# A projection matrix folded four row tiles at a time, output columns in two equal halves, and a new hand-written order of steps

## The chip, the cores and the metric

One Trainium2 chip, one core. The metric is the device time of one execution in microseconds (us). Kernels are compared by the median of several executions. The core's engines run side by side, each through a queue of its own in order: TensorE (PE in the rows; PEld is its weight load), VectorE (DVE), ScalarE (ACT), GpSimd (POOL), and SyncE (SP), whose queue issues the DMAs.

## The reference

Three stages follow one another; r, k, v, w are (4 batches, 8 heads, 768 steps, 48), w_in and w_out come in float64.

```
# 1 attention with a decaying state, per batch and head
y[t] = r[t] @ (state + (u*k[t]) v[t]^T);  state = w[t]*state + k[t] v[t]^T
x = y as (3072 tokens, 384)
# 2 a wide layer
h = x @ w_in          # 384 -> 2048
g = h * cos(h)
x2 = g @ w_out        # 2048 -> 384
# 3 soft mixture of 8 experts with 4 slots each
logits = x2 @ phi                          # 384 -> 32
d = softmax(logits, over tokens);  slot_in = d.T @ x2
slot_out[e] = relu(slot_in[e] @ w1[e]) @ w2[e]
out = softmax(logits, over slots) @ slot_out   # (3072, 384)
```

## The kernel before, in words

**Stages.** x2 itself is never formed. The kernel computes p = w_out @ phi once (2048 x 32, `p_sb`), so that logits are g @ p, and it gathers d.T @ g (`E`, 32 x 2048) and multiplies that by w_out at the end. Attention runs over 24 blocks of 128 tokens (`wT`, `wf`, `scan`, `kT`, `ks`, `rT`, `L`, `A`, `mask`, `U`, `z`, `st`, `y`; the number behind a step's name is the block). The wide layer runs over 12 groups of 256 tokens and 8 blocks of 256 hidden columns: `h.g.i.mm` is one 128-column half of block i in group g, of nine f32r matmuls (L451 to L453: high and low parts of x and w_in). `turns`, `rest`, `cos`, `mul` (ACT, DVE, ACT, DVE) make g, `gT` transposes it, `gc` copies it, `l` adds to the logits. A block of h waits for the `mul` of the block two before it, whose bank it takes.

**The fold and the decode.** The float64 weights are read as pairs of integers and turned into float32 by `abs`, `mx`, `d1`, `d2a`, `d2b` (one on ACT, four on DVE; `i` is w_in, `o` is w_out, each in 8 pieces). For w_out each of 16 row tiles m is then transposed (`oT.m`, L416, three 128x128 pieces), copied to SBUF (`oc.m`, L421, ACT) and multiplied by phi (`om.m`, L427): the transposed tile is the stationary operand, and phi's 32 columns move. All sixteen results lie in one PSUM bank `pp`, held from the first `om` to the last `ps` (L430, ACT), which copies four tiles of it to `p_sb`.

**The order.** A string `HEAD` of some 1980 steps gives the order in which the steps are issued, and with it each engine's queue. Nothing reorders it later. It starts with attention and decode and ends with the last `E`.

**The tail.** After `HEAD` come the slots, then for each expert `hidden` (w1) and `expert_out` (w2, L826, by four column groups of 32 slots), then `slots_out` (L833), `slots_round`, and `outputs` (L857 for 512 tokens in f32, L859 for the others in f32r), whose result is copied from PSUM to `ob` (L866 and L873) and sent (L867). This is done for two parts of the 384 columns: 256, then 128. Five of the w2 weights (`we`) are issued late, into buffers that the wide layer frees.

Of the kernel before, what the change touches and what calls it, by code (L numbers as in the profile page):

```python
# [902 lines left out]
A.0 z.0.1 mask.0 wn.0.0 raw.o.0 st.0.1 lk.2 kT.1 rz.0.1 rz.0.0 lv.1 mx.o.3 d1.o.3 ks.1 d2a.o.3 wn.0.1 wc.0.1 d2b.o.3 lw.2 y.0 lz.2
abs.o.0 lr.2 lw.3 z.1.0 lv.2 A.1 yb.0 mx.o.0 d1.o.0 abs.o.2 mx.o.2 wc.0.0 kN.1 ksn.1 d2a.o.0 d2b.o.0 oT.1 xh.0 xl.0 d1.o.2 raw.i.1
abs.o.1 mx.o.1 d1.o.1 oT.0 oc.0 oc.1 om.0 d2a.o.1 d2a.o.2 wT.2 wf.2 d2b.o.1 om.1 lz.1 raw.i.4 mask.1 d2b.o.2 oT.3 oT.2 oc.2 oc.3
U.1 ru.1 bo.1 oT.4 rz.1.0 abs.i.1 st.1.0 z.1.1 rz.1.1 st.1.1 bv.1 scan.2 kT.2 abs.i.4 om.2 ks.2 y.1 yb.1 om.3 mx.i.4 xh.1 xl.1
mx.i.1 d1.i.1 d2a.i.1 kN.2 d2b.i.1 h.0.2.0 h.0.2.1 ksn.2 oc.4 rT.2 sr.2 sp.2 L.2 raw.i.3 lr.3 lw.4 d1.i.4 z.2.0 d2a.i.4 d2b.i.4
whi.1 wn.1.0 h.0.0.0 wc.1.0 h.0.0.1 turns.0.0 rz.2.0 oT.5 wT.3 oc.5 rest.0.0 ru.2 bo.2 bv.2 U.2 wf.3 A.2 cos.0.0 wn.1.1 st.2.0
turns.0.2 wc.1.1 mul.0.0 gT.0.0 om.4 lk.3 kT.3 mask.2 z.2.1 st.2.1 scan.3 ks.3 rest.0.2 whi.4 abs.i.3 mx.i.3 d1.i.3 sr.3 d2a.i.3
d2b.i.3 sp.3 wn.4.0 kN.3 ksn.3 wn.4.1 h.0.1.0 h.0.1.1 wc.4.0 lw.5 raw.i.6 abs.i.6 lv.4 whi.3 gc.0.0 lk.4 mx.i.6 cos.0.2 wc.4.1  # L910
wn.3.0 oT.7 wc.3.0 rT.3 wn.3.1 raw.i.5 d1.i.6 rz.2.1 oc.7 y.2 wc.3.1 d2a.i.6 turns.0.1 abs.i.5 mul.0.2 L.3 A.3 wT.4 h.0.3.0
d2b.i.6 wf.4 mx.i.5 d1.i.5 z.3.0 whi.6 mask.3 wn.6.1 ps.0 wc.6.1 rest.0.1 scan.4 yb.2 om.5 cos.0.1 xh.2 kT.4 d2a.i.5 ru.3 lk.5
wn.6.0 mul.0.1 sr.4 lv.3 ks.4 l.0.1 xl.2 sp.4 d2b.i.5 U.3 st.3.0 raw.i.7 abs.i.7 z.3.1 mx.i.7 oT.6 wc.6.0 gT.0.2 gc.0.2 lr.5 bo.3
st.3.1 d1.i.7 oc.6 d2a.i.7 h.0.3.1 gT.0.1 wT.5 wf.5 kN.4 h.0.4.0 gc.0.1 d2b.i.7 lz.3 whi.7 wn.7.0 whi.5 h.0.4.1 wn.5.1 lr.4
raw.o.5 bv.3 turns.0.3 rest.0.3 rz.3.0 scan.5 ksn.4 wn.5.0 turns.0.4 rest.0.4 wc.7.0 raw.o.4 lz.4 abs.o.4 mx.o.4 wc.5.0 wc.5.1
rz.3.1 ru.5 bo.5 rT.4 L.4 cos.0.4 om.7 ru.4 wn.7.1 lr.6 om.6 cos.0.3 d1.o.4 d2a.o.4 mul.0.3 ps.1 wc.7.1 abs.o.5 U.4 z.4.0 rz.4.0
st.4.0 z.4.1 st.4.1 rz.4.1 d2b.o.4 y.3 mul.0.4 l.0.3 A.4 yb.3 xh.3 kT.5 ks.5 mask.4 h.0.5.0 xl.3 h.0.5.1 lw.6 lk.6 raw.o.6 rT.5
mx.o.5 lz.5 d1.o.5 turns.0.5 kN.5 ksn.5 sr.5 rest.0.5 oT.8 gT.0.3 oc.8 oT.9 sp.5 d2a.o.5 gc.0.3 bo.4 oc.9 d2b.o.5 cos.0.5 h.0.7.0
h.0.7.1 lv.5 bv.5 turns.0.7 wT.6 om.9 wf.6 mul.0.5 gT.0.5 rest.0.7 L.5 oT.11 raw.o.7 U.5 A.5 oc.11 om.11 z.5.0 scan.6 st.5.0
abs.o.6 mx.o.6 z.5.1 lw.7 abs.o.7 d1.o.6 d2a.o.6 st.5.1 rz.5.1 om.8 cos.0.7 z.6.0 d2b.o.6 mul.0.7 h.0.6.0 h.0.6.1 wT.7 oT.10  # L920
h.1.1.0 h.1.1.1 mask.5 tab turns.0.6 gc.0.5 rest.0.6 gT.0.4 kT.6 cos.0.6 oc.10 sr.6 sp.6 mul.0.6 ks.6 oT.13 oc.13 rz.5.0 om.10
gc.0.4 ps.2 wf.7 rT.6 mx.o.7 d1.o.7 h.1.0.0 oT.12 oc.12 d2a.o.7 d2b.o.7 close l.0.5 om.13 oT.14 oT.15 om.12 turns.1.1 bv.4 ru.6
# [136 lines left out]
```

## Time and profile before

| | before |
|---|---|
| median of 3 runs | 566.48 us (565.99 to 566.79) |
| profiled execution | 567.16 us |
| its span, first to last instruction | 565.4 us |
| mean granted TensorE clock | 0.975 |
| PE busy, share of the span | 516.0 us, 91% |
| DVE busy | 438.7 us, 78% |
| ACT busy | 313.3 us, 55% |
| POOL busy | 123.2 us, 22% |
| read from HBM, written | 61.75 MB, 4.72 MB |

The span leaves out 1.76 us of the execution's own time. Busy shares are means over the span; the start, the long middle and the tail have different limits, so that a change is weighed in its own stretch. A granted clock of 1.00 is 2.4 GHz, one of 0.50 is 1.2 GHz.

### The profile page before, as it was taken

The numbers are of one execution on the slowest core, as the hardware profiler recorded it, in microseconds if no ns is written. First come the engines' busy times: TensorE is split into PE (matmuls) and PEld (weight loads), VectorE is DVE, ScalarE is ACT, GpSimd is POOL, SyncE is SP. The second block draws the span as 40 slices with busy tenths as digits, with TensorE's granted clock in tenths as the row PEclk, the third lists the DMA queues.
The fourth block names the chain that finished last, engine by engine and source line by source line (L and its number), as shares of the span: only waits on it lengthen the run. The fifth ranks groups of instructions, "written<-read, shape, count | busy, mean of one in ns | idle before, by whom it ended". The sixth has DMA issues, their size and how long they took to land.

```text
span 565.4 us, 16220 instructions
## 1 busy us (share of the span) xinstructions
PE 516.0 (91%) x6846; PEld 447.6 (79%) x6846; DVE 438.7 (78%) x823; ACT 313.3 (55%) x657; POOL 123.2 (22%) x163
## 2 busy tenths in 40 slices
...
GB/s 206 297 167 88 144 179 126 128 71 16 112 55 75 68 33 58 44 72 43 45 86 39 61 16 90 41 106 51 59 59 12 6 225 378 180 237 225 405 202 275
DMA packets 146712, 67.52 MB, mean 119 GB/s; under 512 B 127568, under 2 KB 134736, under 8 KB 146640
## 3 DMA queue, kind: packets, MB, share of 16 engines
...
HBM read 61.75 MB, written 4.72 MB: 118 GB/s over the span
## 4 chain that ended last, share of the span: by engine, by line
PE 58%; DVE 27%; ACT 6%; DMA 4%; issue 3%; SPq 0%; DVEq 0%; ACTq 0%
PE h L451 9%; PE h L453 8%; PE h L452 8%; PE gT L483 5%; PE l L496 3%; PE y L288 3%; PE E L592 3%; DVE g L475 3%; DMA we<-in_moe_w_dram 3%; PE A L208 3%; DVE L L222 3%; DVE g L467 3%; DVE L L187 2%; PE U L259 2%; DVE qt L156 2%
## 5 line engine op out<-in xcount | busy, mean ns | idle before, releaser
L451 PE MATMUL h<-x,wu 128*128 128x256 f32 x573 | 168.8, 295 | 3.9 <-DVE g L475 3.6
L453 PE MATMUL h<-x,wu 128*128 128x256 f32 x573 | 162.3, 283 | 0.0
L452 PE MATMUL h<-x,wu 128*128 128x256 f32 x573 | 162.3, 283 | 0.0
L451 PEld LDWEIGHTS h<-x,wu 128*128 128x128 f32 x573 | 110.3, 193 | 6.1 <-DVE g L475 5.2
L452 PEld LDWEIGHTS h<-x,wu 128*128 128x128 f32 x573 | 110.4, 193 | 0.2
L453 PEld LDWEIGHTS h<-x,wu 128*128 128x128 f32 x573 | 110.0, 192 | 0.0
L471 ACT ACTIVATE g<-g,half_pi 128x512 f32<-128x512 f32 (+1 forms) x97 | 69.2, 718 | 44.0 <-DVE g L467 43.4
L463 ACT ACTIVATE g<-h 128x512 int32<-128x512 f32 x96 | 56.9, 595 | 59.1 <-PE h L453 39.1
L467 DVE SCALAR_TENSOR_TENSOR g<-g,h 128x512 f32<-128x512 int32 x96 | 64.9, 678 | 27.5 <-ACT g L463 26.8
L475 DVE TENSOR_TENSOR g<-g,h 128x512 f32<-128x512 f32 x96 | 64.7, 678 | 22.9 <-ACT g L471 22.2
L251 POOL TENSOR_TENSOR bv<-vz,bo 64x384 f32<-64x384 f32 x48 | 41.9, 873 | 151.8 <-DVE bo L243 56.6
L488 ACT COPY gt<-gT 128x512 f32<-128x512 f32 x92 | 53.4, 584 | 28.5 <-PE gT L483 22.5
L483 PE MATMUL gT<-cs,g 128*128 128x128 f32 x384 | 58.9, 278 | 2.4 <-DVE g L475 1.7
L169 POOL TENSOR_TENSOR ru<-rn,u_b 128x384 f32<-128x384 f32 x24 | 27.7, 1156 | 123.2 <-DVE bo L243 46.0
L483 PEld LDWEIGHTS gT<-cs,g 128*128 128x128 f32 x384 | 43.6, 142 | 12.3 <-issue 6.5
L274 ACT COPY rzs<-z 64x192 f32<-64x192 f32 x96 | 33.4, 348 | 9.5 <-DVE z L269 8.4
L156 DVE TENSOR_TENSOR_SCAN qt<-wf,one_b 128x520 f32<-128x520 f32 x24 | 31.9, 1329 | 6.5 <-ACT wf L151 6.4
L187 DVE TENSOR_TENSOR L<-rT,pt 64x512 f32<-64x512 f32 x48 | 32.9, 686 | 4.3 <-PE y L288 2.8
L222 DVE TENSOR_TENSOR L<-A,cs 64x512 f32<-64x512 f32 x48 | 33.1, 689 | 1.2
L193 POOL MEMSET L<- 64x512 f32 x32 | 16.6, 520 | 69.3 <-PE y L288 68.3
L496 PE MATMUL l<-g,p_sb 128*32 128x256 f32 x384 | 29.8, 385 | 1.5 <-DVE g L475 1.5
L164 DVE TENSOR_TENSOR_SCAN pt<-wf,ini_f 128x520 f32<-128x520 f32 x24 | 30.2, 1258 | 0.2
...
## 6 DMA issues: line engine op xcount, KB each, us to landing
...
```

The lines of the kernel that those rows point to most:

```text
L187: nc.vector.tensor_tensor(out=L[h, a], in0=ps[h], in1=segs(pt, 0, C)[h], op=ALU.mult)
L222: nc.vector.tensor_tensor(out=L[h, a], in0=ps[h], in1=mask[h].unsqueeze(1).to_broadcast([64, NS, C]), op=ALU.mult)
L451: nc.tensor.matmul(hp, lhsT=wh, rhs=xh[:, c, :], start=(c == 0), stop=False)
L452: nc.tensor.matmul(hp, lhsT=wh, rhs=xl[:, c, :], start=False, stop=False)
L453: nc.tensor.matmul(hp, lhsT=wl, rhs=xh[:, c, :], start=False, stop=(c == KD - 1))
L463: nc.scalar.activation(gt.bitcast(I32), hp, AF.Copy, bias=0.25, scale=1.0 / TWO_PI)
L467: nc.vector.scalar_tensor_tensor(out=gt, in0=gt.bitcast(I32), scalar=-TWO_PI, in1=hp, op0=ALU.mult, op1=ALU.add)
L471: nc.scalar.activation(gt, gt, AF.Sin, bias=half_pi[:, 0:1])
L475: nc.vector.tensor_tensor(out=gt, in0=gt, in1=hp, op=ALU.mult)
L483: nc.tensor.transpose(ps[:, tt, mm, :], gt[:, mm, tt * 128:(tt + 1) * 128], ident)
L488: (nc.vector.tensor_copy if NBK * g + i >= ATT and i in (1, 2) else nc.scalar.copy)(t, pend.pop(("gT", g, i)))
L496: nc.tensor.matmul(lps_t[g][32 * mm:32 * mm + 32, 0:G], lhsT=p_sb[:, m, :], rhs=g_t[g, m // 2][:, m % 2, :], start=(m < 4), stop=(m >= MF ...
```

## The change

Three things, of which the first two can be seen in the code. **The fold**: `om.u` now takes four row tiles at once. phi is the stationary operand (32 columns), the transposed w_out tile moves with its 128 columns, and the four tiles go to four column groups of the array, which write four quarters of the partitions of a bank `pt` of their own. The result is p transposed, so that two steps follow: `pc` (copy to SBUF, ACT) and `pT` (one transpose); `ps` then copies as before. The transposed tiles lie in the pool of 12 buffers that also holds the copied `gT`. **The tail**: `halves` of 192 columns each take the place of the parts of 256 and 128, the second half's `expert_out` stands alternately with the first half's `outputs`, and the second half's output is stored for every pair of token tiles. **The order**: `HEAD` is another list, of 1977 steps.

```diff
     def e_oc(m):
-        wt_t[m] = aw.tile([128, KD, 128], F32, tag="wt", name=f"wt{m}")
+        wt_t[m] = gt_p.tile([128, KD, 128], F32, tag="gt", name=f"wt{m}")
         nc.scalar.copy(wt_t[m], pend.pop(("woT", m)))
-    def e_om(m):
-        if not pt_ps:
-            pt_ps[0] = ps_m.tile([128, MF, SL], F32, tag="m", name="pp")
+    def e_om(u_):
+        ps = ps_m.tile([128, 512], F32, tag="m", name=f"pt{u_}")
         for c in range(KD):
-            nc.tensor.matmul(pt_ps[0][:, m, :], lhsT=wt_t[m][:, c, :], rhs=phi_sb[:, c, :], start=(c == 0), stop=(c == KD - 1))
+            for q in range(4):
+                nc.tensor.matmul(ps[32 * q:32 * q + 32, 0:128], lhsT=phi_sb[:, c, :], rhs=wt_t[4 * u_ + q][:, c, :], start=(c == 0), stop=(c == KD - 1))
+        pt_ps[u_] = ps
+    def e_pc(u_):
+        wt_t["p", u_] = aw.tile([128, 128], F32, tag="pts", name=f"pts{u_}", bufs=1)
+        nc.scalar.copy(wt_t["p", u_], pt_ps[u_][:, 0:128])
+    def e_pT(u_):
+        pend["P", u_] = tps(f"P{u_}")[:, 0:128]
+        nc.tensor.transpose(pend["P", u_], wt_t["p", u_], ident)
     def e_pw(u_):
-        nc.scalar.copy(p_sb[:, 4 * u_:4 * u_ + 4, :], pt_ps[0][:, 4 * u_:4 * u_ + 4, :])
+        nc.scalar.copy(p_sb[:, 4 * u_:4 * u_ + 4, :], pend.pop(("P", u_)).rearrange("p (q s) -> p q s", q=4))
...
         parts = (slice(0, 256), slice(256, DM))
+        halves = (slice(0, DM // 2), slice(DM // 2, DM))
...
             def expert_out(i, e):
-                cols = parts[i]
+                cols = halves[i]
...
             def outputs(i, n0, tile_=None):
-                cols = parts[i]
+                cols = halves[i]
...
             outputs(0, 1, 0)
             outputs(0, 1, 1)
-            for n0 in range(2, 5):
-                outputs(0, n0)
-            for e in range(1, 4):
+            outputs(0, 2)
+            for e in range(1, NE):
+                outputs(0, e + 2)
                 expert_out(1, e)
-            for n0 in range(5, 9):
-                outputs(0, n0)
-            for e in range(4, NE):
-                expert_out(1, e)
-            nc.vector.tensor_copy(so[:, parts[1]], ops[1][:, 0:128])
-            for n0 in range(9, 12):
-                outputs(0, n0)
+            nc.vector.tensor_copy(so[:, halves[1]], ops[1][:, 0:DM // 2])
+            outputs(0, NE + 2)
             slots_out(1)
+            outputs(0, NE + 3)
             slots_round(1)
-            for n0 in range(6):
+            for n0 in range(12):
                 outputs(1, n0)
...
-z.0.0 lw.0 wT.0 wf.0 scan.0 raw.i.0.0 abs.i.0.0 mx.i.0.0 sr.0 d1.i.0.0 sp.0 raw.i.2 abs.i.2 mx.i.2 raw.i.0.1 abs.i.0.1 lw.1 wT.1
+lw.0 wT.0 wf.0 scan.0 sr.0 lk.0 sp.0 lr.0 kT.0 ks.0 rT.0 lw.1 wT.1 wf.1 raw.i.0.0 abs.i.0.0 raw.i.2 abs.i.2 z.0.0 L.0 A.0 scan.1
```

What the new list does to a queue is shown at three places. In these rows a name is followed by its tile's number. First DVE, where the start ends: the rows around `mul.0.7` (the product that writes `g0_7`, for which `h.1.1.0` waits). Before:

```order
L269 TENSOR_TENSOR z5_0_1335<-st_state_130,qt5_1034 128x192
L156 SCALAR_TENSOR_TENSOR qt6_1337<-wf_127,one_b_128 128x520
L277 TENSOR_TENSOR st_state_130<-U5_1304,z5_0_1335 128x192
L357 TENSOR_SCALAR ao6_1340<-ao6_1340 128x768
L269 TENSOR_TENSOR z5_1_1343<-st_state_130,qt5_1034 128x192
L361 TENSOR_SCALAR ao6_1340<-ao6_1340 128x768
L366 SCALAR_TENSOR_TENSOR ao6_1340<-rawo6_1203,ao6_1340 128x768
L277 TENSOR_TENSOR st_state_130<-U5_1304,z5_1_1343 128x192
L266 MEMSET z6_0_1357 128x192
L374 SCALAR_TENSOR_TENSOR wo_sb_106<-rawo6_1203,ao6_1340 128x768
L475 TENSOR_TENSOR g0_7_1277<-g0_7_1277,h0_7_1253 128x512
L222 TENSOR_TENSOR L5_1295<-A5_1313,cs_103 64x512 x2
```

And now:

```order
L486 TENSOR_TENSOR g0_6_1300<-g0_6_1300,h0_6_1259 128x512
L357 TENSOR_SCALAR ao7_1326<-ao7_1326 128x768
L478 SCALAR_TENSOR_TENSOR g0_7_1241<-g0_7_1241,h0_7_1168 128x512
L361 TENSOR_SCALAR ao7_1326<-ao7_1326 128x768
L366 SCALAR_TENSOR_TENSOR ao7_1326<-rawo7_1321,ao7_1326 128x768
L269 TENSOR_TENSOR z5_0_1392<-st_state_130,qt5_1048 128x192
L374 SCALAR_TENSOR_TENSOR wo_sb_106<-rawo7_1321,ao7_1326 128x768
L156 SCALAR_TENSOR_TENSOR qt6_1451<-wf_127,one_b_128 128x520
L243 TENSOR_REDUCE bo5_1457<-ru5_1429 128x8
L222 TENSOR_TENSOR L5_1349<-A5_1375,cs_103 64x512 x2
L160 RECIPROCAL ini_f_129<-qt6_1451 128x8
L486 TENSOR_TENSOR g0_7_1241<-g0_7_1241,h0_7_1168 128x512
```

The decode of the last piece of w_out (`ao7`), the mask of block 5 (L222), `sr.6` (L160) and the other half of the wide layer's block 0.6 (`rest` and `mul`) now stand ahead of `mul.0.7`; the states of block 5 (L277) and `z.6.0` (L266) are behind it.

Then PE around `h.1.1.0` (the rows that write `h1_1`). Before:

```order
L141 MATMUL wT7_1380<-cs_103,wn1_122 128x128 x4
L416 MATMUL woT10_1385<-cs_103,wo_sb_106 128x128 x3
L451 MATMUL h1_1_1389<-x01_115,wu0_262 128x256
...
L483 MATMUL gT0_4_1416<-cs_103,g0_4_1041 128x128 x4
L141 MATMUL kT6_1421<-cs_103,kn0_119 128x128 x4
L416 MATMUL woT13_1435<-cs_103,wo_sb_106 128x128 x3
L427 MATMUL pp_433<-phi_sb_105,wt10_1427 128x32 x3
L141 MATMUL rT6_1450<-cs_103,rn0_117 128x128 x4
L451 MATMUL h1_0_1457<-x01_115,wu0_262 128x256
```

And now:

```order
L494 MATMUL gT0_6_1407<-cs_103,g0_6_1300 128x128 x4
L462 MATMUL h1_0_1412<-x01_115,wu0_334 128x256
...
L416 MATMUL woT15_1453<-cs_103,wo_sb_106 128x128 x3
L507 MATMUL l0_896<-g0_4_894,p_sb_107 32x256 x2
L507 MATMUL l0_896<-g0_5_1107,p_sb_107 32x256 x2
L429 MATMUL pt3_1467<-wt12_1405,phi_sb_105 32x128
...
L141 MATMUL kT6_1501<-cs_103,kn0_119 128x128 x4
L141 MATMUL wT7_1515<-cs_103,wn1_122 128x128 x4
L494 MATMUL gT0_7_1520<-cs_103,g0_7_1241 128x128 x4
L462 MATMUL h1_1_1527<-x01_115,wu0_334 128x256
```

All of the fold's products (L429, formerly L427) and transposes of w_out (L416), the transposes of g of four blocks (L494, formerly L483), those of k of block 6, the first half of `l.0.5`'s group and the whole of `h.1.0` stand ahead of `h.1.1.0` now; before, `om` of the tiles 10 and 12 to 15 and much of the rest stood behind it. Only the transpose `pT.3` of the fold is still behind it.

Last SP's queue of DMAs at the very start. Before:

```order
L636 DMA cs_103<-in_const_dram 128x320
L116 DMA wn0_121<-in_w_dram 128x8x48
L338 DMA rawi0_168<-in_moe_w_in_dram 128x3x256
L338 DMA rawi2_177<-in_moe_w_in_dram 128x3x512
L338 DMA rawi0b_182<-in_moe_w_in_dram 128x3x256
L116 DMA wn1_122<-in_w_dram 128x8x48
L123 DMA vz0_123<-in_v_dram 64x8x48 x2
L116 DMA kn0_119<-in_k_dram 128x8x48
```

And now:

```order
L647 DMA cs_103<-in_const_dram 128x320
L116 DMA wn0_121<-in_w_dram 128x8x48
L116 DMA kn0_119<-in_k_dram 128x8x48
L116 DMA rn0_117<-in_r_dram 128x8x48
L116 DMA wn1_122<-in_w_dram 128x8x48
L338 DMA rawi0_190<-in_moe_w_in_dram 128x3x256
L338 DMA rawi2_194<-in_moe_w_in_dram 128x3x512
```

Three loads of attention (k and r of block 0, w of block 1, 192 KB each) now stand ahead of the first load of w_in.

## Rows read from the trace of the kernel before

**Rows 1.** Busy time by engine, from the page's first part.

```profile
PE 516.0 (91%) x6846; PEld 447.6 (79%) x6846; DVE 438.7 (78%) x823; ACT 313.3 (55%) x657; POOL 123.2 (22%) x163
```

**Rows 2.** Busy time by stretch; last three columns: granted clock, DMA share, GB/s.

```profile
core 0: us, PE busy (x) PEld busy (x) DVE busy (x) ACT busy (x) POOL busy (x), PEclk, DMA share, GB/s
36.00:123.00 87.00, 73.07 (x793) 62.01 (x793) 78.37 (x117) 47.63 (x92) 22.33 (x20) 0.90 0.59 137
123.00:140.00 17.00, 16.79 (x271) 15.40 (x271) 12.90 (x19) 10.17 (x20) 0.00 (x0) 0.90 0.05 10
140.00:500.00 360.00, 351.71 (x4807) 317.05 (x4806) 292.42 (x577) 211.82 (x451) 82.86 (x102) 1.00 0.37 83
```

**Rows 3.** PE's longest waits from 123 to 500: us in total, times, longest.

```profile
PE h L451 <- DVE g L475: 3.6, 3, 1.5
```

**Rows 4.** PE where the start ends: start us, us, instructions, idle before.

```profile
123.01 0.39 PE L451 MATMUL h<-x,wu 128*128 128x256 f32 x1 [1.19 <-DVE g L475]
```

**Rows 5.** DVE from 120.7 to 132, the timeline.

```profile
120.80 0.35 DVE L277 TENSOR_TENSOR st_state<-U,z 128x192 f32<-128x192 f32 x1
121.33 0.22 DVE L266 MEMSET z<- 128x192 f32 x1 [0.17 <-DVE st_state L277]
...
122.28 0.68 DVE L475 TENSOR_TENSOR g<-g,h 128x512 f32<-128x512 f32 x1
122.98 1.39 DVE L222 TENSOR_TENSOR L<-A,cs 64x512 f32<-64x512 f32 x2
124.30 0.67 DVE L467 SCALAR_TENSOR_TENSOR g<-g,h 128x512 f32<-128x512 int32 x1
124.89 0.19 DVE L160 RECIPROCAL ini_f<-qt 128x8 f32<-128x8 f32 x1
...
126.27 0.66 DVE L475 TENSOR_TENSOR g<-g,h 128x512 f32<-128x512 f32 x1
...
128.51 0.55 DVE L357 TENSOR_SCALAR ao<-ao 128x768 f32<-128x768 f32 x1
...
131.55 1.23 DVE L156 TENSOR_TENSOR_SCAN qt<-wf,one_b 128x520 f32<-128x520 f32 x1
```

**Rows 6.** The fold's matmuls: all of them by line, and a run of 12.

```profile
L427 PE MATMUL pp<-phi_sb,wt x96: 191/276/401, 36.0 to 135.6; 128*128 128x32 f32 x96
134.45 1.42 PE L427 MATMUL pp<-phi_sb,wt 128*128 128x32 f32 x12
```

**Rows 7.** PE from 501.5 to 503.5, the timeline: plain and column-group matmuls.

```profile
501.52 0.28 PE L452 MATMUL h<-x,wu 128*128 128x256 f32 x1
501.64 0.28 PE L453 MATMUL h<-x,wu 128*128 128x256 f32 x1
501.85 1.07 PE L496 MATMUL l<-g,p_sb 128*32 128x256 f32 x16
```

**Rows 8.** Two stretches of the start, by the columns of rows 2.

```profile
8.00:13.00 5.00, 1.09 (x4) 0.72 (x4) 3.84 (x6) 1.80 (x3) 0.00 (x0) 1.00 1.20 178
38.90:48.90 10.00, 9.16 (x107) 8.31 (x107) 6.89 (x12) 4.46 (x9) 4.48 (x4) 0.50 0.50 139
```

**Rows 9.** The tail in the chain that ended last: start us, us, what.

```profile
518.34 2.18 PE E L592 x30
...
528.61 15.46 DMA we<-in_moe_w_dram
```

**Rows 10.** PE's expert and output matmuls after the last weights, the timeline.

```profile
551.34 1.95 PE L826 MATMUL so<-we,wo_sb 128*32 128x128 f32 x64
...
555.43 2.45 PE L859 MATMUL o<-sr,cr 96*128 96x128 f32 x20
```

**Rows 11.** Two stretches of the tail, by the columns of rows 2.

```profile
551.00:553.00 2.00, 2.00 (x64) 1.87 (x66) 1.02 (x2) 1.05 (x2) 0.00 (x0) 1.00 1.03 335
559.00:563.00 4.00, 0.00 (x0) 0.00 (x0) 0.00 (x0) 0.00 (x0) 0.00 (x0) 0.75 1.05 289
```

More of the change, by code (lines that the diff above doesn't have):

```diff
@@ L903 @@
[L903 to L922, printed above, removed]
@@ L987 @@
-st.21.1 mul.8.7 kN.22 gT.8.0 l.8.5 ksn.22 U.22 z.22.0 turns.8.6 rest.8.6 st.22.0 A.22 ru.22 bo.22 scan.23 gc.8.0 lv.23 lz.22
-rz.22.0 cos.8.6 mul.8.6 sr.23 z.22.1 rz.22.1 kT.23 gT.8.5 h.9.0.0 h.9.0.1 turns.9.0 bv.22 ru.23 st.22.1 h.9.1.0 h.9.1.1 cmb.0.5
-ks.23 rest.9.0 mask.22 gc.8.5 gT.8.7 kN.23 rz.21.0 y.21 y.22 l.8.7 cos.9.0 mul.9.0 lz.23 z.23.0 gc.8.7 ksn.23 U.23 turns.9.1
-rest.9.1 cos.9.1 gT.8.6 mul.9.1 sum.8 rz.23.0 yb.22 xh.22 gc.8.6 h.9.3.0 lc.8 gT.9.0 yb.21 xh.21 h.9.3.1 turns.9.3 gc.9.0 xl.22
@@ new lines @@
+cos.2.0 rz.7.1 ru.8 lk.10 rT.8 mask.7 kN.8 ksn.8 gT.2.1 h.2.3.0 h.2.3.1 mul.2.0 h.2.2.0 h.2.2.1 turns.2.3 gc.2.1 sum.1 lw.10 lr.10
+wT.9 gT.1.7 zl.8 L.8 l.2.1 A.8 wT.10 bo.8 rest.2.3 cos.2.3 mul.2.3 h.2.4.0 h.2.4.1 wf.9 turns.2.2 rest.2.2 cos.2.2 scan.9 mul.2.2
+gc.1.7 sr.9 sp.9 wf.10 turns.2.4 lc.1 gT.2.0 gc.2.0 max.1 exp.1 lk.9 rest.2.4 h.2.5.0 h.2.5.1 xt.1 xr.1 xd.1 U.8 y.7 l.2.3 bv.8
+lw.12 lz.9 cos.2.4 turns.2.5 rest.2.5 mul.2.4 st.8.0 z.8.1 st.8.1 zl.9 dT.1 yb.7 xh.7 cos.2.5 mul.2.5 gT.2.3 gc.2.3 ru.9 h.2.6.0
@@ new lines @@
+scan.11 bo.10 sum.2 cos.3.0 sr.11 h.3.2.0 h.3.2.1 mul.3.0 gT.2.4 gc.2.4 lc.2 max.2 mask.10 wT.12 turns.3.2 exp.2 h.3.3.0 h.3.3.1
+sp.11 ksn.10 rz.9.1 rest.3.2 kT.11 ks.11 gT.3.1 gc.3.1 cos.3.2 mul.3.2 l.3.1 lr.11 ru.11 lv.10 lk.13 y.9 yb.9 gT.3.0 xh.9 bo.11
+xt.2 turns.3.3 rest.3.3 xr.2 xl.9 h.3.4.0 h.3.4.1 wf.12 xd.2 gc.3.0 gT.2.7 bv.11 rT.11 cos.3.3 mul.3.3 turns.3.4 gc.2.7 dT.2
+rest.3.4 U.10 ltok.2 cos.3.4 dc.2 cmb.0.0 mul.3.4 z.10.0 cmb.0.1 cmb.0.4 gT.3.3 gc.3.3 h.3.5.0 h.3.5.1 kN.11 lr.12 turns.3.5 ru.12
@@ new lines @@
+zl.11 L.11 rest.3.5 st.10.0 l.3.3 cos.3.5 E.2.0 E.2.1 gT.3.2 z.10.1 ksn.11 h.3.7.0 h.3.7.1 lz.10 rz.10.1 turns.3.7 gc.3.2 lr.13
+st.10.1 mul.3.5 z.11.0 bv.10 lv.12 lz.11 rest.3.7 cos.3.7 cmb.0.2 es.2 mul.3.7 h.3.6.0 h.3.6.1 turns.3.6 rz.11.0 rest.3.6 cos.3.6
+A.11 U.11 cmb.0.3 st.11.0 gT.3.5 rz.10.0 kT.12 z.11.1 st.11.1 rz.11.1 h.4.0.0 h.4.0.1 gc.3.5 l.3.5 y.10 zl.12 scan.12 mul.3.6
+turns.4.0 rest.4.0 ks.12 sr.12 z.12.0 l.3.7 mask.11 gT.3.4 cos.4.0 lw.14 mul.4.0 yb.10 xh.10 sp.12 h.4.1.0 gc.3.4 sum.3 h.4.1.1
```

195 lines of the change are left out of this document (103 added, 92 removed).

## The prediction

> **What bounds the kernel now.** The page's totals come first [rows 1]: PE is busy 91% of the span, DVE 78%. That is a mean over unlike stages, so the second view is busy time by stretch [rows 2]. From 36 to 123 us DVE is busy 78.37 of 87 us (90%) while PE has 73.07: attention and the decode of the weights fill DVE, PE waits for it, and the start is paced by DVE. From 123 to 140 PE is busy 16.79 of 17, and from 140 to 500 it is busy 351.71 of 360 at a granted clock of 1.00: from 123 on PE paces. The third view, PE's waits, confirms it: its largest wait after 123 is 3.6 us in three pieces [rows 3]. The handover is one instruction. `h.1.1.0` starts at 123.01, after PE stood idle for 1.19 us, released by the product of L475 [rows 4], which DVE ran from 122.28 for 0.68 us [rows 5]. That product is `mul.0.7`.
>
> This gives a rule to reckon by. Up to the handover, what counts is how much DVE has to do before `mul.0.7`; behind it, how much PE still has to do. Work that moves on DVE from behind the handover to ahead of it costs its time; work that moves on PE from behind to ahead saves its time, as long as it fits into PE's idle time, of which the stretch before has 87 - 73.07 = 13.9 us [rows 2].
>
> The fourth view is the chain that ended last. The last `E` starts at 518.34 and takes 2.18 us; then the slots and the first layer of the experts follow, and a transfer of w2 weights, 15.46 us from 528.61, is waited for [rows 9]. Those transfers start when the buffers of the wide layer come free, so they move with the end of the wide layer, and so does the tail behind them. At the very end PE, DVE and ACT show nothing from 559 to 563 while the DMA share is 1.05 at 289 GB/s [rows 11]: the end of the tail is paced by its output DMAs.
>
> **The change, part by part.**
>
> *The handover, DVE.* The order's rows show what now stands ahead of `mul.0.7` that stood behind it: the mask of block 5 (122.98 to 124.30, 1.32 us), `rest.0.6` (to 124.89, 0.59), `sr.6` (0.19), `mul.0.6` (0.66), and the decode of the last piece of w_out, four instructions from 128.51 to 131.55 (3.04) [rows 5]. Together 5.80 us. Behind it go two updates of the state at 0.35, one step `z.5.1` that I price like them, and a memset of 0.22 [rows 5]: 1.27. Net +4.5 us: I expect `mul.0.7` to end at 122.96 + 4.5 = 127.5.
>
> *The handover, PE.* Of the fold, 30 of its 96 records (two per f32 matmul; `om` of tiles 10 and 12 to 15, three matmuls each) stood behind `h.1.1.0` and now all of it is ahead. Twelve of them started in a row from 134.45 within 1.42, the last taking some 0.19 [rows 6], so (1.42 - 0.19)/11 = 0.11 apart; with the switches within such a run left out I take 0.104: 3.1 us. `h.1.0` (18 matmuls, 0.12 from start to start [rows 7]) moves ahead: 2.2. So do 28 transposes (three blocks of g and the k of block 6 at four each, four tiles of w_out at three each) of the same 128x128 weight load, priced at the same 0.12: 3.4. `l.0.5` is 8 records of column groups, 16 of which take 1.0 [rows 7]: 0.5. `pT.3` is now behind: +0.1. Net 9.1 us less behind the handover, all of it in place of PE's idle time or of the fold's own saving ahead of it. The first term is so 4.5 - 9.1 = **-4.6 us**.
>
> *The fold's new form.* phi becomes the stationary operand and four column groups work at once. Nothing in the trace has this form with 128 moving columns but the experts: 64 records of `expert_out`, 128 columns in four groups, in 1.95 us, 0.0305 each [rows 10]. Ninety-six records at that price are 2.9 us instead of 96 x 0.104 = 10.0; four transposes of p at 0.12 come on top: PE has 6.6 us less in all. The upper bound for a record is the old 0.104 (nothing gained), the lower 0.0305; I take the lower, the same shape. Since all of it lies ahead of the handover, where DVE paces, neither end changes the sum beyond the 3.1 us counted above. ACT gets four copies more; it is busy 47.63 of 87 us there [rows 2].
>
> *A rule on column groups.* Entering the groups costs a little in this trace: `h` matmuls start 0.12 apart, the first of `l` 0.21 after the last `h` [rows 7], so about 0.09 a switch, and 8 switches for four `om` come to 0.7 us. The Trainium skill, "TensorEngine Tiling (Array Packing)", Tiling Modes, Key Properties, says that changing the tiling mode drains TensorE. By that rule a switch would cost the whole of a matmul in flight, 0.28 - 0.12 = 0.16, so 1.3 us. The trace agrees in kind, less in size, and either sum would be hidden ahead of the handover.
>
> *The start.* On SP three loads of 192 KB stand ahead of the first load of w_in. At the 178 GB/s of 8 to 13 us [rows 8] that is 576 KB / 178 = 3.2 us later for the decode of w_in. What covers it is DVE's work of attention that now stands ahead of the decode (`ks.0`, `L.0`, `scan.1`, about 0.7 + 1.4 + 1.2 = 3.3 by like rows [rows 5]). I put it at nothing; without cover it is +3.2, with early attention well used it is a small gain.
>
> *The middle.* Steps change places, but each `h` has the same matmuls, and PE is busy 98% there [rows 2]. The total of PE's work behind the handover apart from the above is the same. Reordered waits could give or take a microsecond; I put zero.
>
> *The tail.* Two equal halves of 192 columns make the DMA rows 768 bytes instead of 1024 and 512. The trace gives 335 GB/s where rows of 1024 go out and 289 where rows of 512 do [rows 11]; half way is 312. The 4.72 MB take the same either way within 0.3 us. But `expert_out(1, e)` now stands between outputs: PE must do two output matmuls (0.12 each [rows 10]) and 16 records for an expert, 0.0305 each at 128 columns and by columns 0.046 at 192: 0.24 + 0.73 = 0.97 us for 197 KB, which the DMAs send in 0.63. Seven such steps starve them by 0.3 each, 2.1 us. Before, two blocks of experts stood between the outputs, the longer of 1.95 us with the DMAs still at a share of 1.03 [rows 10, 11]; for the pauses around both I estimate 1.2 us. On the other side the first half is ready sooner, 16 experts' records of 192 columns instead of 256. I take **+0.7**, between -0.5 (the first output 0.4 earlier, no starving) and +1.5 (all of it). If f32r outputs of 192 columns run more slowly than 0.12, +0.5 more.
>
> *Sum.* 567.16 - 4.6 + 0.7 = 563.3 for the profiled execution, which stood 0.68 above the median of the runs shown; so 562.6.
>
> **The rivals.**
>
> *DVE's start gets tighter as well.* DVE idles 8.6 of the 87 us from 36 to 123 [rows 2]. A new list that interleaves attention and decode differently could win back half, 4.3 us more: 558.3. For it: each idle piece there is a wait for ACT, PE or a transfer, and early attention gives DVE more to choose from. Against it: the list has as much DVE work before the same point by count, and its DMAs start later.
>
> *PE's relief is lost in waits.* The work moved ahead of the handover might not fit into PE's idle pieces, since its inputs come late: the last decode now ends just before `mul.0.7`, and `oT.14`, `oT.15`, `om.3` wait for it. Then PE does them all between the decode and `h.1.1.0` and the handover moves by as much. The first term is nothing, and the time about 567.16 + 0.7 - 0.68 = 567.2.
>
> *Slower: the clock.* From 38.9 to 48.9 PE ran at a granted clock of 0.50, half speed, after it had waited, and was yet busy 9.16 of 10 us [rows 8]. The fold makes PE emptier before the handover, and each wait there can be followed by such a stretch. If one more like it falls where PE paces, just behind the handover, PE does 10 us of work at half speed in it, 5 us lost, and waits 0.84 us more (10 - 9.16): 562.6 + 5.8 = 568.4. It ends slower than before by more than can be told apart once 5.0 us are lost, that is a stretch of some 8.6 us.
>
> **How the numbers follow.** Forecast 0.46, DVE tighter 0.20, relief lost 0.16, clock 0.18. The forecast's own range is 560 to 565.3: tail from -0.5 to +2.0, start from -1 to +1.5. The range over the cases is 556.5 to 568.5. About 0.2% or 1.13 us is what a measurement of this kernel can tell from no change: 565.35 to 567.61. The forecast and the tighter start end faster (0.66, less 0.02 for the forecast's own slips), relief lost falls within it, the clock lies above it, but a tenth of its cases within. Faster 0.64, same 0.18, slower 0.18.
>
> **What would show it.** `mul.0.7` ends at about 127.5 and `h.1.1.0` starts right behind it; the last `E` ends near 520.5 - 4.6 = 516; the fold has 96 records some 0.03 apart in four runs, all of them before the handover. In the tail the DMA share between the first half's outputs dips while `expert_out(1, e)` runs, and the last output comes some 45 to 46 us behind the last `E`. If `mul.0.7` ends earlier than 126, the tighter start is right. If PE's stretch before `h.1.1.0` is full and DVE waits for it, the relief was lost. If the granted clock is 0.5 behind the handover for 5 us or more, it is the clock. The prediction is wrong above all if DVE's idle time before the handover grows, for then every later stage moves with it.

## The result, and the profile after

The changed kernel takes 570.36 us (median of 5 runs, 568.31 to 570.85), the kernel before 566.36 (5 runs, 565.46 to 566.79): a ratio of 1.0074, with a 95% interval of 1.0049 to 1.0099. It is slower, by some 4 us; I had forecast 562.6. Measured again later beside other kernels, the ratio was 1.0100 (1.0075 to 1.0125). The profiled execution took 570.54 us, with a span of 568.6 and a mean granted clock of 0.971.

The start and the middle by stretch, as in [rows 2]:

```profile
core 0: us, PE busy (x) PEld busy (x) DVE busy (x) ACT busy (x) POOL busy (x), PEclk, DMA share, GB/s
36.00:123.00 87.00, 74.27 (x871) 58.97 (x872) 82.98 (x129) 54.21 (x108) 27.09 (x20) 0.96 0.61 137
123.00:140.00 17.00, 16.49 (x280) 15.28 (x279) 13.79 (x24) 10.82 (x25) 3.72 (x5) 1.00 0.26 50
140.00:500.00 360.00, 346.07 (x4741) 310.96 (x4740) 287.49 (x567) 211.56 (x447) 84.96 (x98) 1.00 0.34 78
```

The start went better than forecast: from 36 to 123 DVE is busy 82.98 of 87 us where it was 78.37. The middle went worse: PE is busy 346.07 of 360 us where it was 351.71, so that 5.6 us more are idle there. From 123 to 140 the granted clock is 1.00 where it was 0.90 [rows 2]: before, PE ran at half speed just behind the handover, which the prediction left out:

```profile
124.20:127.40 3.20, 3.20 (x17) 3.20 (x16) 2.70 (x5) 1.58 (x3) 0.00 (x0) 0.50 0.00 0
```

The handover, on the timelines of DVE and PE:

```profile
120.70 0.64 DVE L486 TENSOR_TENSOR g<-g,h 128x512 f32<-128x512 f32 x1
```
```profile
119.29 1.40 PE L429 MATMUL pt<-wt,phi_sb 128*32 128x128 f32 x24
...
122.36 0.60 PE L494 MATMUL gT<-cs,g 128*128 128x128 f32 x4
122.72 0.36 PE L462 MATMUL h<-x,wu 128*128 128x256 f32 x1
125.39 0.27 PE L438 MATMUL P<-cs,pts 128*128 128x128 f32 x1
```

`mul.0.7` ended at 121.34, not at 127.5, with the longer list of work ahead of it, and `h.1.1.0` started at 122.72 straight behind other PE work (123.01 after a wait in [rows 4]). So PE stood 0.3 us earlier at the same instruction with less work behind it. How much less, two stretches show, from `h.1.1.0` to `dT.11` (the transpose that the last `E` waits for), before and then after:

```profile
123.01:517.49 394.48, 383.74 (x5225) 344.19 (x5225) 316.17 (x621) 234.56 (x502) 83.69 (x103) 1.00 0.37 89
```
```profile
122.72:516.10 393.38, 375.10 (x5149) 336.32 (x5148) 311.05 (x615) 232.62 (x494) 89.79 (x104) 1.00 0.36 87
```

PE is busy 8.6 us less, and idles 18.28 us where it idled 10.74, 7.5 more.

So the list behind gave most of it back. PE's waits from 123 to 500, by line and what ended them:

```profile
PE y L288 <- issue: 3.1, 1, 3.1
PE kT L141 <- ACT wf L151: 1.6, 1, 1.6
PE l L507 <- DVE g L486: 1.3, 1, 1.3
PE gT L494 <- ACT gt L499: 1.3, 2, 0.7
```

The largest is put down to "issue", that is to nothing which the profile shows. The timeline of all engines around it, and the stretch behind it, tell what it is:

```profile
450.22 1.05 PE L507 MATMUL l<-g,p_sb 128*32 128x256 f32 x16
450.90 1.08 ACT L474 ACTIVATE g<-h 128x512 int32<-128x512 f32 x2 [5.00 <-PE l L507]
451.53 1.28 DVE L478 SCALAR_TENSOR_TENSOR g<-g,h 128x512 f32<-128x512 int32 x2 [4.91 <-ACT g L474]
...
453.49 0.71 ACT L274 COPY rzs<-z 64x192 f32<-64x192 f32 x2
...
454.36 1.93 PE L288 MATMUL y<-L,rzs 128*32 128x64 f32 x64 [3.09 <-issue]
```
```profile
454.20:457.60 3.40, 3.24 (x75) 2.46 (x76) 3.23 (x11) 0.59 (x1) 0.00 (x0) 0.51 0.00 0
```

`turns.9.7` (ACT, L474) waits 5.0 us for `l.9.5` on PE, which must free a buffer of g. Everything behind it on ACT and DVE then runs late, `rz.23.1` (L274) among it, which `y.23` reads; PE, whose queue is in order, stands still until then. Behind the wait PE ran at half speed for 3.4 us, which cost some 1.6 more. The start of the tail follows, PE's timeline:

```profile
512.35 0.60 PE L520 MATMUL lc<-lg,cs 128*128 128x256 f32 x2
...
516.10 0.47 PE L579 MATMUL dT<-cs,dl 128*128 128x128 f32 x1 [2.69 <-ACT dl L551]
517.09 3.64 PE L603 MATMUL E<-gt,dt 128*32 128x256 f32 x32 [0.51 <-ACT dt L586]
...
522.28 4.58 PE L779 MATMUL si<-wo_sb,et 128*32 128x256 f32 x64
```
```profile
515.80:525.80 10.00, 9.11 (x75) 4.39 (x79) 3.54 (x13) 2.44 (x9) 0.00 (x0) 0.50 0.40 136
```

PE waits 2.69 us before `dT.11` (1.56 before the change), and from 515.8 to 525.8 its granted clock is 0.50 (1.2 GHz): the last `E` takes 3.64 us where it took 2.18 [rows 9]. In the chain of before, `dT.11` and the first output started here:

```profile
517.49 0.34 PE dT L568
...
545.67 0.70 PE o L857 x2
```

After, they start at 516.10 and 545.78. Last the outputs, PE's timeline and stretches of 2 us, then longer ones, after and before:

```profile
545.78 0.59 PE L869 MATMUL o<-wo_sb 128*128 128x192 f32 x2
...
550.54 0.86 PE L838 MATMUL so<-we,wo_sb 128*32 128x192 f32 x16
551.33 0.47 PE L871 MATMUL o<-sr,cr 96*128 96x192 f32 x2
551.72 0.86 PE L838 MATMUL so<-we,wo_sb 128*32 128x192 f32 x16
```
```profile
551.00:553.00 2.00, 2.00 (x36) 1.13 (x32) 0.21 (x1) 0.48 (x1) 0.00 (x0) 1.00 0.61 190
553.00:555.00 2.00, 2.00 (x35) 1.16 (x36) 0.56 (x1) 0.48 (x1) 0.00 (x0) 1.00 0.40 123
```
```profile
549.00:559.00 10.00, 9.82 (x130) 6.86 (x127) 3.14 (x7) 2.71 (x6) 0.00 (x0) 1.00 0.64 199
```
```profile
549.00:557.00 8.00, 7.89 (x150) 7.17 (x141) 4.15 (x8) 3.27 (x7) 0.00 (x0) 1.00 0.93 301
```

A pair of tiles and an expert take PE 1.18 us (550.54 to 551.72), and the DMA share falls to 0.40 and 0.61 in two of the stretches. While the first half's outputs go out it is 0.64 on average, where it was 0.93. From the first output to the end it is 568.6 - 545.78 = 22.8 us, where it was 565.4 - 545.67 = 19.7.

The span's 3.2 us then add up: `dT.11` comes 1.4 us earlier, the way from it to the first output is 1.5 longer (29.68 beside 28.18), and the outputs are 3.1 longer.

### The profile page after: what moved, and what is told of

It is laid out like the page before. It is cut to its first block, busy times and chain, and to the rows that moved or that the text cites. A ratio compares the mean times of both kernels' runs of the same rounds, so it can differ in the third digit from the quotient of the medians.

```text
span 568.6 us, 16266 instructions
## 1 busy us (share of the span) xinstructions
PE 515.3 (91%) x6850; PEld 440.4 (77%) x6850; DVE 436.2 (77%) x826; ACT 315.4 (55%) x664; POOL 134.4 (24%) x163
## 4 chain that ended last, share of the span: by engine, by line
PE 60%; DVE 23%; ACT 9%; issue 3%; DMA 2%; SPq 1%; DVEq 0%; ACTq 0%
PE h L462 8%; PE h L464 8%; PE h L463 8%; PE gT L494 6%; PE l L507 3%; PE E L603 3%; PE A L208 3%; PE y L288 3%; PE U L259 2%; DVE g L478 2%; DVE L L222 2%; DVE g L486 2%; ACT g L482 2%; PE so L838 2%; PE hps L798 2%
## 5 line engine op out<-in xcount | busy, mean ns | idle before, releaser
L474 ACT ACTIVATE g<-h 128x512 int32<-128x512 f32 x96 | 56.7, 596 | 65.7 <-PE h L464 37.2
L251 POOL TENSOR_TENSOR bv<-vz,bo 64x384 f32<-64x384 f32 x48 | 46.6, 972 | 106.7 <-DVE bo L243 26.9
L499 ACT COPY gt<-gT 128x512 f32<-128x512 f32 x92 | 53.5, 584 | 25.6 <-PE gT L494 22.8
L494 PE MATMUL gT<-cs,g 128*128 128x128 f32 x384 | 59.2, 278 | 4.4 <-DVE g L486 2.3
L169 POOL TENSOR_TENSOR ru<-rn,u_b 128x384 f32<-128x384 f32 x24 | 31.4, 1309 | 126.0 <-DVE bo L243 58.1
L494 PEld LDWEIGHTS gT<-cs,g 128*128 128x128 f32 x384 | 43.3, 141 | 14.8 <-issue 4.4
L274 ACT COPY rzs<-z 64x192 f32<-64x192 f32 x96 | 33.4, 348 | 9.5 <-DVE z L269 8.6
L156 DVE TENSOR_TENSOR_SCAN qt<-wf,one_b 128x520 f32<-128x520 f32 x24 | 30.2, 1257 | 7.9 <-ACT wf L151 7.7
L222 DVE TENSOR_TENSOR L<-A,cs 64x512 f32<-64x512 f32 x48 | 33.1, 689 | 3.6 <-PE A L208 2.6
L288 PE MATMUL y<-L,rzs 128*32 128x64 f32 x1536 | 28.3, 229 | 5.2 <-issue 3.1
L288 PEld LDWEIGHTS y<-L,rzs 128*32 128x32 f32 x1536 | 25.5, 115 | 9.4 <-issue 4.2
## 6 DMA issues: line engine op xcount, KB each, us to landing
we<-in_moe_w_dram SPq DMA_DIRECT2D x16, 1536.0 KB, 10.2
```

Of the source, the lines that this page charges most:

```text
L251: nc.gpsimd.tensor_tensor(out=bv[h], in0=vn_t[j][h, :, c, :], in1=bo[h].to_broadcast([64, H, D]), op=ALU.mult)
L288: nc.tensor.matmul(ps[m:m + 32, o, c * C:(c + 1) * C], lhsT=rz[:, c, p, a, 32 * b:32 * b + 32], rhs=L[:, a, 2 * p + c, :], start=m not in ...
L474: nc.scalar.activation(gt.bitcast(I32), hp, AF.Copy, bias=0.25, scale=1.0 / TWO_PI)
L494: nc.tensor.transpose(ps[:, tt, mm, :], gt[:, mm, tt * 128:(tt + 1) * 128], ident)
L499: (nc.vector.tensor_copy if NBK * g + i >= ATT and i in (1, 2) else nc.scalar.copy)(t, pend.pop(("gT", g, i)))
```

## The experiments

Twelve of the fifteen kernels ask where the loss is; the last three follow up on what stayed open. Each was timed against the kernel before on its own chip, whose median there was 565.0 to 566.2 us; ratios are to that, with 95% intervals. Of a list the fences show the steps around the edit, and `...` marks code that is left out.

**1. New front, old rest.** The changed kernel's list up to `h.1.1.1`, then the steps still open in the order of before.

```diff
 h.1.1.1
-rest.1.0 st.5.1 wf.7 kN.6 cos.1.0 turns.1.1 mul.1.0 pT.3 ps.3 rT.6
+bv.5 st.5.1 z.6.0 tab wf.7 rT.6 turns.1.1 scan.7 rest.1.1 y.5 lz.7
```

> The changed kernel with its own list up to h.1.1.1 and, for all steps still open there, the order of the list of before. Theory (the list behind the handover gives the gain back): PE is 9 us ahead at the handover and the old order keeps most of it; the granted clock stays 1.00 through the last E; about 558 us. Rival (a middle that is so full can't keep a lead: PE then waits for DVE whatever the order): 565 to 568 us, with PE idle 6 to 8 us more between 123 and 517 than before.

565.3 us, ratio 0.9986 (0.9963 to 1.0008). Its profiled execution took 1228.4 us, more than twice any other, and stands neither in the ratio nor in a row. The kernel is 0.9% faster than the changed kernel, so the list behind the handover does cost; but it is not the 558 of the theory.

**2. Old front, new rest.** The reverse, on the code of before.

```diff
 h.1.1.1
-mask.5 tab turns.0.6 gc.0.5 rest.0.6 gT.0.4 kT.6 cos.0.6
+oc.10 turns.0.6 rest.0.6 bv.4 lv.6 oT.13 oc.13 om.10 gc.0.5 cos.0.6
```

> The kernel before, old fold and old tail, with its own list up to h.1.1.1 and the new list's order for all steps still open there. Theory (the new order's waits are its own): 8 us more idle time in the middle and a low clock at the last E, 574 to 578 us. Rival (the waits come only of PE being early): 566 to 569 us.

582.48 us, ratio 1.0293 (1.0254 to 1.0331), beyond the theory. The wait of 3.1 us before `y.23` and that of 2.7 before `dT.11` stand in it unchanged, though none of PE's work was moved ahead of the handover: they are the list's own. Beside them PE ran at half speed in two stretches around the handover:

```profile
120.70:124.10 3.40, 3.40 (x18) 3.40 (x18) 0.31 (x1) 0.00 (x0) 0.00 (x0) 0.50 0.09 13
134.40:141.20 6.80, 6.80 (x67) 6.14 (x70) 2.89 (x4) 3.11 (x7) 0.00 (x0) 0.50 0.01 2
```

That is 10.2 us at half speed, 5.1 lost, where the kernel before has one such stretch of 3.2 us, 1.6 lost. The 3.5 us between them the theory had not in it.

**3 and 4. The tail alone.** The changed kernel with the tail of before, and the kernel before with the new tail.

```diff
 def expert_out(i, e):
-    cols = halves[i]
+    cols = parts[i]
...
```

> The changed kernel with the tail of before (256 and 128 columns, two blocks of experts between outputs). Theory: the new tail costs 0.7 us, so 569.6 beside 570.4 of the changed kernel. Rival (the tail costs the whole loss): 566.

> The kernel before with the new tail alone (two halves of 192 columns). Theory: +0.7 us, 567.1 beside 566.4. Rival (the new tail is the loss): 570. Other rival (it is a gain that the list hides): 565.

567.41 us, ratio 1.0022 (0.9992 to 1.0051); and 568.44, ratio 1.0056 (1.0030 to 1.0082). Taken out, the tail gives 0.52%, some 2.9 us; put in, it costs 0.56%, some 3.2, each with an interval of some 2 us to either side. Both miss what I had carried over from the prediction, 0.7, and agree with each other. From the first output to the end the profiles show 19.7 us with the old tail and 22.8 with the new, whichever the list.

**5. Filling the wait before the last `dT`.** The extra matmuls' results are not used.

```diff
+        for _ in range(5 if g == NG - 1 else 0):
+            nc.tensor.matmul(ps[:, 256:512], lhsT=ident, rhs=wo_sb[:, 0, 0:256], start=True, stop=True)
         nc.tensor.transpose(ps[:, 0:4 * SL], dl[g % 2][:, 0:2 * QT], ident)
```

> The changed kernel with five f32 matmuls (128x128 by 256 columns, about 0.43 us each) into an unused part of dT.11's bank, issued on PE just ahead of dT.11, whose results nobody reads: they fill 2.1 of the 2.7 us in which PE waits there. Theory (the low clock at the last E and the slots follows that wait): no stretch at 0.50 from 515.7, E.11 takes 2.2 instead of 3.6 us and the slots 2.8 instead of 4.6; 567.1 us. Rival (the clock falls for another reason): 570.4, still 0.50.

568.06 us, ratio 1.0044 (1.0019 to 1.0069). PE's timeline:

```profile
512.33 2.32 PE L580 MATMUL dT<-wo_sb,cs 128*128 128x256 f32 x10
515.18 0.33 PE L581 MATMUL dT<-cs,dl 128*128 128x128 f32 x1 [0.53 <-ACT dl L551]
516.02 1.93 PE L605 MATMUL E<-gt,dt 128*32 128x256 f32 x32 [0.51 <-ACT dt L588]
...
519.39 2.81 PE L781 MATMUL si<-wo_sb,et 128*32 128x256 f32 x64
```
```profile
515.20:525.00 9.80, 9.05 (x143) 5.79 (x147) 4.90 (x18) 4.41 (x13) 2.02 (x1) 1.00 0.58 213
```

With PE kept busy the clock stays at 1.00, `E.11` takes 1.93 us and the slots 2.81. From `dT.11` to the first output it is 542.92 - 515.18 = 27.74 us beside 29.68: work that is of no use saved 1.9 us there. `E.11` and the slots save 3.5, but PE now waits 1.6 us for the last w2 weights (in the changed kernel it doesn't wait there): part of what is won lies beside those transfers. The ratio is 0.3% or 1.7 us below the changed kernel's 1.0074, whose interval it overlaps, and 0.6% below that of its second measurement, whose interval it just misses.

**6 and 12. The wait before `y.23`.** First its inputs (`rz.23.1` and `mask.23`) earlier, then `E.8` behind `l.9.5` too. The fence shows the twelfth; the sixth leaves `E.8` in its place.

```diff
-A.23 E.8.0 E.8.1 l.9.3 cos.9.4 mul.9.4 l.9.5 turns.9.7
+A.23 l.9.3 cos.9.4 mul.9.4 rz.23.1 mask.23 l.9.5 E.8.0 E.8.1 turns.9.7
```

> The changed kernel with rz.23.1 and mask.23 moved in the list to just behind mul.9.4, so that they no longer stand behind turns.9.7, which waits for l.9.5 to free a buffer of g. Theory (y.23's 3.1 us of PE idle at 451 come from this queue): the wait is gone, and the stretch at 0.50 from 454.2 too; 565.7 to 567.5. Rival (PE, once early, waits just as long somewhere behind): 570.

> The changed kernel with rz.23.1 and mask.23 behind mul.9.4 as in the sixth experiment, and E.8.0 and E.8.1 (1.9 us of PE) moved from ahead of l.9.3 to behind l.9.5, so that l.9.5 frees the buffer of g for turns.9.7 1.9 us sooner and PE has E.8 to do meanwhile. Theory (PE waits there for the chain turns, rest, cos, mul of block 9.7): the wait at l.9.7, 2.2 us in the sixth experiment, falls below 0.5; 565 to 566 us. Rival: it comes back at another place, 567.4.

567.44 us, ratio 1.0034 (1.0016 to 1.0052); and 565.85, ratio 0.9995 (0.9972 to 1.0018). PE's wait there in the sixth, then in the twelfth:

```profile
PE l L507 <- DVE g L486: 2.2, 1, 2.2
```
```profile
PE l L507 <- DVE g L486: 0.6, 1, 0.6
```

Moving the inputs alone moved the wait to `l.9.7`, which hangs on the same chain. Moving PE's work between the release and the chain's end removed it. With these two moves the changed kernel is as fast as the kernel before, its costly tail included. They gain 0.8%, some 4.5 us, more than the wait of 3.1; the granted clock there is 1.00 from 453 to 461, where it had been 0.51 for 3.4 us.

**7 and 8. The fold alone.** The new list with the old form of the fold, and the old list with the new form.

```diff
-om.2 L.5
+om.8 om.9 om.10 om.11 L.5
...
```

> The changed kernel with the old form of the fold (transposed w_out stationary, phi moving, one bank), four om where the one om.u stands, without pc and pT. Theory (the fold's form lies ahead of the handover and is hidden): 570 to 571, with PE busier by 5 to 7 us ahead of 122.7. Rival (the fold's form carries the earlier handover): 574 to 577.

> The kernel before with the new form of the fold alone: om.u where the last of its four om stood, pc.u behind it, pT.u just ahead of ps.u. Theory: 30 of 96 records behind the handover become cheaper by 0.05 to 0.07, 1.5 to 2 us less, 564.5. Rival (the waits for pc and pT cost as much): 566.4 or more.

574.57 us, ratio 1.0152 (1.0110 to 1.0194, without the run of 580.9); and 567.94, ratio 1.0059 (1.0030 to 1.0089). In the new list the old form costs 0.8% (some 4 us) beside the first measurement of the changed kernel and 0.5% beside the second, whose interval it overlaps. The seventh's trace tells why, first the end of `mul.0.7` on DVE, then PE:

```profile
120.93 0.63 DVE L475 TENSOR_TENSOR g<-g,h 128x512 f32<-128x512 f32 x1
```
```profile
119.93 2.87 PE L427 MATMUL pp<-phi_sb,wt 128*128 128x32 f32 x24
...
124.82 0.36 PE L451 MATMUL h<-x,wu 128*128 128x256 f32 x1
```

`mul.0.7` ends at 121.56, nearly as early as in the changed kernel (121.34), but `h.1.1.0` starts at 124.82, 2.1 us later than in the changed kernel: the last quarter of the fold takes PE 2.87 us in place of 1.40, a little ahead of it. So the fold's form carries part of the early handover. In the old list the new form doesn't pay: PE waits 2.2 us before one `pT` and 1.1 in all before two others. The form is only worth what the list around it makes of it.

**9. New front, old rest, old tail.** The first and third together.

> The first experiment's list (new up to h.1.1.1, then the order of before) with the tail of before. Theory (three separate parts: the front gains some 8 us of PE work, the new list's rest gives 6.4 us of it back in waits and 1.5 to 2 in clock, the new tail costs 3.1): 565.3 - 3.1 = 562.2 us, with PE idle 12 to 14 us from 122 to dT.11 and 19.7 us from the first output to the end. Rival (the old rest has no use for the lead either): 565 to 566, idle time 18 us or more.

562.3 us, ratio 0.9931 (0.9905 to 0.9956): as the theory had it, faster than both kernels. The tail is additive, within the intervals.

**10. Halves with blocks of experts.**

```diff
-            outputs(0, 2)
-            for e in range(1, NE):
-                outputs(0, e + 2)
+            for n0 in range(2, 5):
+                outputs(0, n0)
+            for e in range(1, 4):
                 expert_out(1, e)
...
```

> The changed kernel, its halves of 192 columns kept, but with expert_out(1, e) for e = 1 to 3 behind outputs(0, 4) and for e = 4 to 7 behind outputs(0, 8), the blocks of before. Theory (the alternation starves the output DMAs, the halves don't matter): 567.5 us, with the first output to the end in 19.7 to 20.3 us. Rival (rows of 768 bytes and 192 columns cost it): 570, 22.8 us.

568.84 us, ratio 1.0048 (1.0027 to 1.0069), between the two; its outputs take 568.6 - 547.36 = 21.2 us. So half of the 3.1 us is the alternation, and half comes with the halves. The size of the second half fits PE's longer blocks, which is an account and was not tested by itself: 112 records of `expert_out` at 192 columns now run between outputs instead of 112 at 128, in 4.97 us (2.16 for 48, 2.81 for 64) instead of 3.47 (1.95 for 64 [rows 10], and 1.52 for 48 in the same trace).

**11. The new list mended, old tail.** The two moves of the twelfth, a third, which the fence shows, and the tail of before.

```diff
-l.11.3 E.10.0 turns.11.7.1 rest.11.7.1 E.10.1
+l.11.3 E.10.0 turns.11.7.1 rest.11.7.1
 lc.11
+E.10.1
```

> The changed kernel with the tail of before, and three moves in its list: rz.23.1 and mask.23 to behind mul.9.4, E.8.0 and E.8.1 to behind l.9.5, E.10.1 to behind lc.11. Theory: tail -3.1, the wait at y.23 and l.9.7 -2.5, E.10.1 fills 1 us of the wait before dT.11 and the clock stays at 1.00 for -1.5 to -2: 562 to 563.5 us. Rival (mended waits come back elsewhere, as they did in the sixth experiment at l.9.7): 566.

562.48 us, ratio 0.9931 (0.9903 to 0.9958), as the theory had it. `E.11` takes 1.93 us.

**13 and 14. The mix mended.** In the ninth PE waits 4.2 us before `pT.3`:

```profile
PE P L438 <- DVE L L187: 4.2, 1, 4.2
```

```diff
-tab wf.7 rT.6 turns.1.1 scan.7 rest.1.1 y.5 lz.7 cos.1.1 rest.1.0 mul.1.1 cos.1.0 mul.1.0 L.6 y.4 pT.3 ps.3
+wf.7 pT.3 ps.3 rT.6 rest.1.0 cos.1.0 mul.1.0 L.6 turns.1.1 scan.7 rest.1.1 y.5 lz.7 cos.1.1 mul.1.1 y.4
```

The fence shows the fourteenth, which also moves `tab`, a table load of 1.28 us on ACT, to behind `turns.8.5`. The thirteenth moves only `pT.3` and `ps.3`.

> The ninth experiment's kernel (new list to h.1.1.1, then the order of before, tail of before) with pT.3 and ps.3 moved ahead of rT.6. In the ninth, PE stood 4.2 us before pT.3, in whose place the granted clock then was 0.50 for 6.8 us. Theory (the wait is of pT.3 alone, whose bank L.6 frees late): the wait goes, 562.3 - 4 to 7 = 555 to 558 us. Rival (PE waits for L.6 itself, which stands on DVE behind mul.1.0): A.6 waits 3 us in its place, 561 to 562 us.

> The thirteenth kernel with rest.1.0, cos.1.0, mul.1.0 and L.6 moved ahead of turns.1.1 and rest.1.1, and tab (a table load on ACT of 1.28 us, followed by another when the sine comes back) moved from there to behind turns.8.5. Theory (L.6 is late by DVE's and ACT's queue): no wait over 1 us before A.6 and no low clock there, 555 to 558 us. Rival: the wait comes back further behind, 561 us.

561.21 us, ratio 0.9931 (0.9906 to 0.9956): no gain over the ninth, for the wait comes back at `A.6`. The fourteenth: 557.79, ratio 0.9869 (0.9845 to 0.9894), the fastest kernel of the study. PE's waits from 120 to 175 in the thirteenth, then in the fourteenth:

```profile
PE A L208 <- DVE L L187: 3.0, 1, 3.0
PE y L288 <- ACT wf L151: 1.0, 1, 1.0
```
```profile
PE lc L520 <- ACT lg L514: 1.8, 1, 1.8
PE A L208 <- DVE L L187: 0.4, 1, 0.4
```

It was `L.6` that was late: it stood behind the work of block 1.1 on DVE, which itself ran late behind `tab` on ACT (DVE waits 1.75 us there for `wf.7`, which stands behind `tab`). The fourteenth moves both, so that it doesn't show their shares. A smaller wait stays at `lc.0`.

**15. The changed kernel again.**

> The changed kernel as it is, on the chip of the two others: 570.4 us as before, 0.7% above the kernel before, with E.11 at a granted clock of 0.50 again in the profile. Rival (the first measurement was a poor draw): within 0.2% of the kernel before.

571.1 us, ratio 1.0100 (1.0075 to 1.0125), with `E.11` again at 3.58 us behind the same wait of 2.69. The first measurement was no poor draw. The slots, though, take 2.81 us here, at full clock: how long half speed lasts differs from one execution to another.

## Why the prediction was wrong

- **The handover** was right in its mechanism and too small. DVE came 6.2 us earlier to `mul.0.7` than forecast. Up to the end of `mul.0.7` these are the stretches, before and after:

```profile
0.00:122.96 122.96, 92.75 (x990) 76.29 (x990) 105.34 (x160) 62.91 (x118) 33.66 (x51) 0.92 0.69 161
```
```profile
0.00:121.34 121.34, 94.68 (x1065) 73.91 (x1065) 106.85 (x165) 66.13 (x128) 37.42 (x49) 0.94 0.74 168
```

Half of it is the mechanism of the first rival: DVE idles 14.5 us there where it idled 17.6. The other half is the count, for its busy time grew by 1.5 us and not by 4.5. Of the second rival a sign is there: from 117.80 to `h.1.1.0` PE is busy throughout, and `mul.0.7` had ended 1.4 us before; that cost part of DVE's gain, not the relief. The forecast term was -4.6; PE's lead was 0.3 + 8.6 = 8.9 us. Of the 9.1 counted, some 0.5 are four transposes (`gT.11.6`) that now stand ahead of `dT.11` and stood behind it; the two stretches at half speed, 3.2 us before at the handover and 3.4 us after at `y.23`, about cancel. The fourteenth experiment shows that such a lead can be kept: it has 351.46 us of PE work from 140 to 500, as before, and is 7 us faster.
- **"Reordered waits could give or take a microsecond; I put zero"** is the step that failed first. They took 7.5 us, 18.28 beside 10.74 from `h.1.1.0` to `dT.11`. I counted the work ahead of the handover and behind it, and priced no queue behind it. Experiments 6 and 12 show one wait of 3.1 us to be a fault of the list (`E.8` ahead of `l.9.5`, and the inputs of `y.23` behind `turns.9.7`), and 2 that such waits come without any work moved ahead. The wait before `dT.11` is 1.1 of the 7.5; the 3.3 left are waits of at most 1.6 us that no experiment takes apart.
- **The tail's +0.7** was mis-sized: it measured 3.1 in the profiles, 2.9 and 3.2 in the medians. The step of the loop took 1.18 us instead of 0.97: 16 records at 192 columns take 0.79, not 0.73, and two outputs with the switches around them 0.39, not 0.24. Seven steps then cost 7 x (1.18 - 0.63) = 3.9 us instead of 2.1. And the 1.2 us which I set against it for the pauses of before were too much: at 0.93 over 8 us the DMA engines stood idle there some 0.6 us, and after, at 0.64 over 10, some 3.6. My upper end of +1.5 was no bound.
- **The clock** was a rival with the right mechanism at the wrong place. It fell not behind the handover but behind the wait before `dT.11`, where it cost 1.9 us by the trace of experiment 5 (1.7 by its median), and behind that before `y.23`, some 1.6, not 5.8.
- **The fold's form.** Its price was about right. The first of its four runs on PE is this one,

```profile
51.30 0.86 PE L429 MATMUL pt<-wt,phi_sb 128*32 128x128 f32 x24
```

and this the copies ahead of the last, on ACT:

```profile
118.96 0.84 ACT L422 COPY wt<-woT 128x384 f32<-128x384 f32 x2
```

The first run's records start (0.86 - 0.27)/23 = 0.026 us apart, as the experts' do ((1.95 - 0.27)/63 = 0.027; the 0.0305 has the last record's end in it). Only the last run, from 119.29, takes 1.40, for it needs those two copies, and the second ends at 119.80. All of it lies ahead of the handover, as forecast. But that the form then changes nothing beyond the 3.1 us counted is not borne out: PE is full just there, and experiment 7 shows 2.1 us in its trace and some 3 to 4 in its median, with a wide interval.
- **The start** needs no correction: the later loads of w_in are not seen in `mul.0.7`.

The sum for the profiled pair is so: handover -0.3, PE's work behind it -8.6, waits +7.5, `dT.11` to first output +1.5, outputs +3.1, together +3.2.
